# Attention and a mixture of experts on one core: the weights that turn values into gate products, made per pair of heads or per batch

## The chip, the cores and the metric

The kernel runs on one core of a Trainium2 chip. The metric is the time of one execution on the device, in microseconds (us). Five engines work side by side, each on its own queue of instructions: TensorE (PE; its weight loads are listed as PEld), VectorE (DVE), ScalarE (ACT), GpSimd (POOL) and SyncE (SP), which here only issues DMAs. Matrix products land in PSUM, in tiles that belong to tags with a fixed number of buffers each; the other engines read them there.

## The reference

Two operations in a row. The first is attention over 8 batches, 8 heads, 576 positions of 64 numbers, with rotated queries and keys:

```python
q_rot, k_rot = (rotate(q), rotate(k))
scores = scale * np.matmul(q_rot, k_rot.transpose(0, 1, 3, 2))
attn = np.exp(scores - np.max(scores, axis=-1, keepdims=True))
attn = attn / (np.sum(attn, axis=-1, keepdims=True) + 1e-09)
x = np.matmul(attn, v)            # to (8*576, 8*64) = (4608, 512) rows
```

The second sends each of the 4608 rows through a dense feed-forward part and through the one of eight experts that a gate names:

```python
logits = x @ w_gate               # (4608, 8)
expert_idx = np.argmax(logits, axis=1)
gate_w = softmax(logits)[row, expert_idx]
out = relu(x @ w1_dense) @ w2_dense
out[row] += gate_w * (relu(x @ w1[e]) @ w2[e])      # e = expert_idx[row]
```

The gate is linear in the attention's output, so it can be applied to the values before the attention weights are: the attention over (values times gate) gives the logits.

## The kernel before

**Pairs, batches, steps.** Two heads are worked on together: a pair. A batch has four pairs (`HP`), the whole attention 32 (`NP`). `attention()` (L657) runs 33 steps, i=0 to 32, each with nine parts t=0 to 8 (L692-693). In step i three pairs are under way:

- `s1_block(i+2, t)`: the scores of pair i+2 by rows of queries (L366), of which VectorE takes the negated row maximum `negm` (L368). Tag s1, two buffers.
- `s2_strip(i, t)`: the scores of pair i, transposed (L389), and their exponential on ScalarE into `pm` (L399). At the end of the step `s2_tails` does the same for the last 64 queries (L386, and an exponential). Tag s2, two buffers.
- `av_part(i-1)`: the product of the exponentials and the values of pair i-1 (L421), ten parts over t=1 to 8, into the PSUM tile `av` (one buffer). At t=8 `av_scale` divides by the row sums on VectorE: `rz` (L432), `xn` (L433), `lw` (L435) and, with the last pair of a batch, so at the end of steps with i%4=0, the sum `lgs` (L438). Its end is also what `av`'s next user, the next step's first part, waits for.

The instructions stand on each engine in just the order in which this loop writes them. Nothing is moved by a scheduler; every engine waits in its queue for what its first instruction needs.

**The row maximum** must be inside the exponent of the transposed scores. `shift_rows(i+1)` (t=1) turns `negm` on TensorE into a tag s2 tile (L374), writes it as two bf16 rows `mT` (ScalarE and VectorE), and SP copies these as rows 126 and 127 into `qT` (L379). There the first strip of the next step needs them.

**Queries and keys.** GpSimd rotates a pair's queries and keys at t=2 of the step five ahead (`stage_rope`, L311 to L314), a transposing DMA turns them into `qT` at t=2 of the step four ahead (`stage_transpose`, L324), and at t=2 of the step three ahead `stage_keys` (L349) lets SP copy the keys' half of `qT` to `kx` (L352), of which there are four buffers. `s1_block` reads `kx` first, one step after that. The raw rows come by `stage_load` at t=2, a quarter of a batch's main rows in each step, in the batch two ahead.

**Values.** The tile `v16s[b % 2]` holds for each of four pairs and five groups of 128 positions, for each of two heads: the values in fp16 (64 columns), two columns that count ones, and 16 columns of gate products: value times gate, as a high part of 8 and a low part of 8 (the high part's rounding). Making them takes these steps:

- `stage_v(b+1)` at t=5 of the batch's first step (i%4=0): SP loads the values of the next batch into `vf`, which has one buffer (L263, and the tails at L266).
- `cast_v(b, u)`: ScalarE copies pair u of them to fp16 (L270). Two casts stand in a step with i%4=0 (t=1 and t=4), one in those with i%4=2 and 3 (t=3), none with i%4=1; the last batch's lie in steps 26 and 27.
- `v_turn(i+1)` at t=5 of every step: TensorE transposes the five groups of the next pair into a tag s2 tile (L277), ScalarE copies it to `vT` (L279).
- `v_gate(i)` at t=1: ten matmuls of `vT` and the gate (high and low part, `wgb`) into free columns of the `av` tile (L287).
- `v_split(i)` at t=2: ScalarE writes the high part into `v16s` (L296), VectorE the low part, the product less the high part (L297). The product of pair i with its values starts at t=1 of the next step, so both are there by then; but they read the `av` tile, and `av_part` of the pair before goes on in the same tile at t=3.

**Other DMAs at t=5.** `x_store(b)` (L115) stores the batch's rows `xn` to DRAM in the steps with i%4=1. The ten weight loads of the second operation stand in GpSimd's queue in the steps `WS`, those of 6 to 23 with i%4=2 and 3.

**The end.** Steps 27 to 31 also route the rows of the first six batches to experts, on VectorE and GpSimd; at step 30 the first rows are gathered (`draw`, L825). From about 323 us on follows the second operation (`ffn`, L895), which the change does not touch.

Of the kernel before, what the change touches and what calls it, by code (L numbers as in the profile page):

```python
# [25 lines left out]
def kernel(  # L26
# [234 lines left out]

    def stage_v(b):
# [10 lines left out]
    def v_turn(p):  # L273
        b, u = divmod(p, HP)
        ps = pp.tile([P, 5, P], fp16, tag="s2", bufs=2, name="vps")
        for n in range(5):
            nc.tensor.transpose(ps[:, n], v16s[b % VB][:, u, n, VA:VA + 2 * D], ident_h)  # L277
        vT = ap.tile([P, 5, P], fp16, tag="vT", bufs=2, name="vT")
        nc.scalar.copy(vT, ps)  # L279
        state["vT", p] = vT  # L280

    def v_gate(p):
        vw = state["av"][:, 1, 5 * VC:5 * VC + 10 * E]
        vT = state.pop(("vT", p))
        for n in range(5):
            for x in range(2):
                nc.tensor.matmul(vw[:, 2 * E * n:2 * E * (n + 1)], lhsT=vT[:, n], rhs=wgb[:, p % HP, x],  # L287
                                 start=(x == 0), stop=(x == 1))
        state["vw", p] = vw

    def v_split(p):

        b, u = divmod(p, HP)
        vw = state.pop(("vw", p)).rearrange("p (n h e) -> p h n e", h=2, e=E)
        hi, lo = (both(v16s[b % VB][:, u, :, r * E:(r + 1) * E], VC + WB) for r in range(2))
        nc.scalar.copy(hi, vw)  # L296
        nc.vector.tensor_tensor(lo, vw, hi, AL.subtract)  # L297
# [359 lines left out]
    def attention():  # L657
# [29 lines left out]
        WS = [i for i in range(6, 24) if i % HP in (2, 3)]  # L687
# [3 lines left out]
        state["av"] = av_tile(0)  # L691
        for i in range(NP + 1):  # L692
            for t in range(9):
# [9 lines left out]
                if t == (7 if i == 0 else 5) and i + 1 < NP:  # L703
                    v_turn(i + 1)
                if i == 0 and t == 2:
                    v_turn(0)
                if i == 0 and t in (3, 5):
                    cast_v(0, 2 + t // 5)
                if i < NP:
                    t0 = 4 if i == 0 else 1  # L710
                    if t == t0:
                        v_gate(i)
                    if t == t0 + 1:
                        v_split(i)
# [4 lines left out]
                if t == 2 and i + KA < NP:  # L719
                    stage_keys(i + KA, nc.sync)  # L720
                if t == 2 and i + LA < NP:
                    stage_transpose(i + LA)
                    nb, m = divmod(i - 1, HP)
                    if 2 <= nb + 2 < B:
                        stage_load(nb + 2, m // 2 * 2, m // 2 * 2 + 2, m % 2, (0, HP) if m < 2 else ())
# [272 lines left out]
```

## Time and profile before

| | us |
|---|---|
| median of three runs | 473.59 |
| lowest, highest | 472.63, 475.58 |
| the profiled execution | 475.16 |
| its span in the trace | 473.4 |

The rows of the profile name an engine, a line, an operation, and what it writes and reads (out<-in by the program's names, with the shape), then how many, the busy time and the mean of one; behind the last bar stands the idle time of the engine before them and what ended most of it. In a timeline each line is one instruction or a few alike (x2, x10): its start, its length, and in brackets how long its engine had waited and for what.

Over the span TensorE is busy for 87%, VectorE for 73%, GpSimd for 72% and ScalarE for 62%. In forty slices of 11.8 us each (busy tenths; the clock granted to TensorE in tenths):

```profile
PE   1787998998988998998888979788999999999992
DVE  7887899999989999999899998943478323232341
ACT  6587787887877887887786875674433133332320
POOL 1899999897998989977997978745266444663232
PEclk9999999999999999999999997999999999999996
```

Attention fills the slices to about the 27th: there VectorE is at 80 to 90% or more, TensorE often not. Behind it, TensorE is at 90% or more to the end. The mean of the clock is 0.985.

### The profile page before, as it was taken

Reading aid. Unit: us, or ns where it says so; the run is one execution under the profiler, and the core shown is the slowest. Engines: PE = TensorE matmul, PEld = TensorE weight load, DVE = VectorE, ACT = ScalarE, POOL = GpSimd, SP = SyncE. Lnnn points to the kernel's source line nnn. Section 1 sums busy time; section 2 is a strip of 40 time slices with the busy share of each in tenths; the row PEclk is TensorE's granted clock in tenths of the full one; section 3 lists DMA queues with packets and bytes.
Section 4 is the critical chain, followed back from the end, with each engine's and each line's share of the span. In section 5 each row is a group of like instructions: output and inputs, shape, how many; then the busy total and the mean of one; then the engine's idle time right before and its main releaser. Section 6 shows DMA issues by size and latency. Waiting matters only on the chain.

```text
span 473.4 us, 11393 instructions
## 1 busy us (share of the span) xinstructions
PE 409.8 (87%) x4256; PEld 255.4 (54%) x4256; DVE 343.9 (73%) x651; ACT 293.9 (62%) x589; POOL 342.8 (72%) x279
## 2 busy tenths in 40 slices
PE   1787998998988998998888979788999999999992
PEld 1345665665655665665665656464445544444550
DVE  7887899999989999999899998943478323232341
ACT  6587787887877887887786875674433133332320
POOL 1899999897998989977997978745266444663232
PEclk9999999999999999999999997999999999999996
DMA  6877648779789779879779639938654556543121
GB/s 186 222 164 156 163 107 223 180 144 237 210 153 242 198 135 245 200 143 249 210 140 230 122 56 199 204 80 183 86 159 134 115 146 155 157 125 123 67 91 69
DMA packets 114124, 75.82 MB, mean 160 GB/s; under 512 B 73332, under 2 KB 107636, under 8 KB 114068
## 3 DMA queue, kind: packets, MB, share of 16 engines
q1 hardware_dynamic: 99556, 51.07, 46.6%
q0 software_dynamic: 14240, 23.73, 23.2%
q8 instruction: 36, 0.59, 0.5%
q10 hardware_dynamic: 272, 0.26, 0.2%
q14 instruction: 20, 0.16, 0.1%
HBM read 52.05 MB, written 14.42 MB: 140 GB/s over the span
## 4 chain that ended last, share of the span: by engine, by line
PE 50%; DVE 24%; DMA 12%; ACT 8%; issue 4%; SPq 1%; POOLq 0%; POOL 0%; DVEq 0%
DVE negm L368 14%; DMA kx<-qT 8%; PE py L885 7%; PE py L883 7%; PE pe L865 7%; PE pd L856 6%; PE av L421 6%; PE s L366 6%; ACT pm L399 5%; PE s L389 4%; DVE xn L433 3%; PE s L362 2%; ACT v L270 2%; PE tr L874 2%; PE s L386 1%
## 5 line engine op out<-in xcount | busy, mean ns | idle before, releaser
L368 DVE TENSOR_REDUCE negm<-s 128x1 f32<-128x576 f32 x288 | 209.9, 750 | 22.3 <-PE s L366 17.1
L399 ACT ACTIVATE pm<-s 128x512 f16<-128x512 f32 x288 | 168.4, 598 | 63.9 <-PE s L389 47.4
L366 PE MATMUL s<-kx,qT 126*128 126x288 bf16 x512 | 108.2, 294 | 21.0 <-DVE negm L368 10.0
L421 PEld LDWEIGHTS <-pm 128*128 128x128 f16 x1600 | 86.9, 98 | 63.0 <-issue 34.6
L389 PE MATMUL s<-qT,kx 128*128 128x64 bf16 (+1 forms) x512 | 109.7, 286 | 2.9 <-ACT pm L399 1.5
L421 PE MATMUL av<-v,pm 128*128 128x82 f16 x1600 | 100.4, 200 | 8.7 <-DVE v L297 8.6
L311 POOL TENSOR_TENSOR ra<-qk,cosx 128x1152 bf16<-128x1152 f32 x30 | 78.8, 2626 | 28.5 <-DVE nat L314 10.7
L888 POOL DMA_INDIRECT out_dram<-y,put_i x37 | 37.9, 1024 | 64.3 <-DVE y L887 42.8
L314 POOL TENSOR_TENSOR nat<-ra,rb 128x1152 bf16<-128x1152 bf16 x30 | 70.9, 2363 | 2.3
L366 PEld LDWEIGHTS <-qT 126*128 126x128 bf16 x512 | 40.4, 99 | 37.6 <-issue 27.4
L887 DVE COPY y<-py 128x512 f32<-128x512 f32 x37 | 25.6, 691 | 42.1 <-PE py L885 42.1
L868 ACT ACTIVATE hn<-pe,gp 128x512 bf16<-128x512 f32 x37 | 25.4, 686 | 46.1 <-PE pe L865 45.3
L820 POOL DMA_INDIRECT xg<-xd,take_i x37 | 36.8, 994 | 20.8 <-issue 9.8
L858 ACT ACTIVATE hd<-pd 128x512 bf16<-128x512 f32 (+1 forms) x40 | 22.6, 565 | 44.8 <-PE py L883 37.8
L876 DVE COPY he<-tr 128x512 bf16<-128x512 bf16 x37 | 15.6, 422 | 38.1 <-PE tr L874 38.1
L312 POOL TENSOR_TENSOR rb<-qk,sinx 128x576 bf16<-128x576 f32 x30 | 42.1, 1403 | 0.0
L313 POOL TENSOR_TENSOR rb<-qk,sinx 128x576 bf16<-128x576 f32 x30 | 42.0, 1398 | 0.0
L389 PEld LDWEIGHTS <-kx 128*128 128x128 bf16 x512 | 35.0, 97 | 8.0 <-issue 1.0
L856 PE MATMUL pd<-xs,w1d 128*128 128x512 bf16 (+1 forms) x160 | 38.0, 363 | 1.3 <-DMA xs<-xg 1.3
L865 PE MATMUL pe<-w1e,xs 128*128 x148 | 38.0, 379 | 0.9 <-PE pd L856 0.6
L883 PE MATMUL py<-w2d,hd 128*128 128x512 bf16 x148 | 38.0, 379 | 0.0
L885 PE MATMUL py<-w2e,he 128*128 x148 | 38.0, 379 | 0.0
(180 smaller groups left out, 484.6 us busy)
## 6 DMA issues: line engine op xcount, KB each, us to landing
vf<-in_v_dram SPq DMA_DIRECT2D x8, 1024.0 KB
qk<-in_q_dram SPq DMA_DIRECT2D x15, 512.0 KB
qk<-in_k_dram SPq DMA_DIRECT2D x15, 512.0 KB
kx<-qT SPq DMA_DIRECT2D x30, 144.0 KB
xd<-xn SPq DMA_DIRECT2D x8, 512.0 KB
w1e<-in_moe_w_dram POOLq DMA_DIRECT2D x8, 512.0 KB, 6.2
w2e<-in_moe_w_dram POOLq DMA_DIRECT2D x8, 512.0 KB, 13.0
vf<-in_v_dram SPq DMA_DIRECT2D x16, 64.0 KB
```

Of the source, the lines that this page charges most:

```text
L311: eng.tensor_tensor(a, x, cx, AL.mult)
L312: eng.tensor_tensor(s[:, :, :, 0:half], x[:, :, :, half:D], sx[:, :, :, 0:half], AL.mult)
L314: eng.tensor_tensor(nat.rearrange("p c w d -> p w c d"), a, s, AL.add)
L366: nc.tensor.matmul(ps[:, c, 0:CH], lhsT=qT[:, t * P:(t + 1) * P], rhs=kT[:, k0 + c * CH:k0 + (c + 1) * CH], start=True, stop=True)
L368: nc.vector.tensor_reduce(state["negm", i][:, t:t + 1], ps[:, :, 0:CH], axis=AX.XY, op=AL.max, negate=True)
L389: nc.tensor.matmul(out_ap, lhsT=kT[:, s * P:(s + 1) * P], rhs=qT[:, qa if s < 4 else qb], start=True, stop=True)
L399: nc.scalar.activation(state["pm", i][:, ORDER.index(s), 0:MAIN], ps, AF.Exp, scale=float(scale))
L421: nc.tensor.matmul(state["av"][:, h, x * VC:(x + 1) * VC], lhsT=state["pm", i][:, 4 * h + n if n < 4 else 8, q0:q0 + P], rhs=v16s[b % VB][ ...
L856: nc.tensor.matmul(ps[:, 0:n], lhsT=w1d[:, dt, ft * P:(ft + 1) * P], rhs=xs[:, 0:n, dt, :], start=(dt == 0), stop=(dt == DT - 1))
L865: nc.tensor.matmul(ps, lhsT=xs[:, u, dt, :], rhs=w[:, 0, dt, :], start=(dt == 0), stop=(dt == DT - 1))
L883: nc.tensor.matmul(py, lhsT=hd[:, ft, u], rhs=w2d[:, ft, :], start=(ft == 0), stop=False)
L885: nc.tensor.matmul(py, lhsT=he[:, ft], rhs=w[:, 0, ft, :], start=False, stop=(ft == FT - 1))
```

## The change

- The gate products of a batch's four pairs are made together, at the end of the step with i%4=0, ahead of the batch's first product with values: forty matmuls into a tag s2 tile of their own, then one copy (ScalarE) and one subtraction (VectorE) for all four pairs, 320 numbers a row in place of four times 80. For the first batch they are made in two halves, at the end of steps 0 and 1. `vT` is now one tile with room for four pairs, with one buffer in place of two.
- So the casts and turns of a batch must be over by t=4 of its step with i%4=0. They are put, by pair, at (i%4, t): (1,6) and (1,8); (2,3) and (2,5); (3,3) and (3,5); (0,2) and (0,4). Batch 1's first turn is at (2,1) instead, batch 7's third and fourth cast stand in step 27. Every step now has one cast and one turn.
- The keys' copy is at t=0 in place of t=2, from step 2 on.
- The raw rows of batches 3 to 7 are loaded one step earlier than before, their tails partly in a step of their own; those of batch 2 as before but for the split of their tails.
- `xn` is stored in the steps with i%4=3 in place of 1 (the seventh batch's in step 29 still).
- The weights are loaded in the steps of 5 to 22 with i%4=1 and 2.

```diff
+    def stage_tails(b, part):
+        load_tails(state["qk", b][:, part], (q, k)[part][b], 0, HP)
...
-    def v_turn(p):
-        b, u = divmod(p, HP)
+    def v_turn(b, u):
+        if u == 0:
+            state["vT"] = ap.tile([P, HP, 5, P], fp16, tag="vT", bufs=1, name="vT")
         ps = pp.tile([P, 5, P], fp16, tag="s2", bufs=2, name="vps")
         for n in range(5):
             nc.tensor.transpose(ps[:, n], v16s[b % VB][:, u, n, VA:VA + 2 * D], ident_h)
-        vT = ap.tile([P, 5, P], fp16, tag="vT", bufs=2, name="vT")
-        nc.scalar.copy(vT, ps)
-        state["vT", p] = vT
-
-    def v_gate(p):
-        vw = state["av"][:, 1, 5 * VC:5 * VC + 10 * E]
-        vT = state.pop(("vT", p))
-        for n in range(5):
-            for x in range(2):
-                nc.tensor.matmul(vw[:, 2 * E * n:2 * E * (n + 1)], lhsT=vT[:, n], rhs=wgb[:, p % HP, x],
-                                 start=(x == 0), stop=(x == 1))
-        state["vw", p] = vw
-
-    def v_split(p):
-
-        b, u = divmod(p, HP)
-        vw = state.pop(("vw", p)).rearrange("p (n h e) -> p h n e", h=2, e=E)
-        hi, lo = (both(v16s[b % VB][:, u, :, r * E:(r + 1) * E], VC + WB) for r in range(2))
-        nc.scalar.copy(hi, vw)
-        nc.vector.tensor_tensor(lo, vw, hi, AL.subtract)
+        nc.scalar.copy(state["vT"][:, u], ps)
+
+    def v_gate(u0):
+        if "vw" not in state:
+            state["vw"] = pp.tile([P, HP * 5, 2 * E], f32, tag="s2", bufs=2, name="vw")
+        for u in range(u0, u0 + 2):
+            for n in range(5):
+                for x in range(2):
+                    nc.tensor.matmul(state["vw"][:, 5 * u + n], lhsT=state["vT"][:, u, n], rhs=wgb[:, u, x],
+                                     start=(x == 0), stop=(x == 1))
+
+    def v_part(b, r, u0=0, u1=HP):
+        vw = (state["vw"] if r == 0 else state.pop("vw"))[:, 5 * u0:5 * u1].rearrange("p n (h e) -> p h n e", h=2)
+        hi, lo = (both(v16s[b % VB][:, u0:u1, :, y * E:(y + 1) * E].rearrange("p u n e -> p (u n) e"), VC + WB)
+                  for y in range(2))
+        if r == 0:
+            nc.scalar.copy(hi, vw)
+        else:
+            nc.vector.tensor_tensor(lo, vw, hi, AL.subtract)
...
-        WS = [i for i in range(6, 24) if i % HP in (2, 3)]
+        WS = [i for i in range(5, 23) if i % HP in (1, 2)]
...
-        state["av"] = av_tile(0)
+        loads = {}
+        for b in range(2, B):
+            n = (b - 2) * HP
+            for at, f, *x in ((n, stage_load, b, 0, 2, 0, ()), (n + 1, stage_load, b, 0, 2, 1, ()),
+                              (n + 1, stage_tails, b, 0), (n + (1 if b == 2 else 2), stage_tails, b, 1),
+                              (n + 2, stage_load, b, 2, 4, 0, ()), (n + 3, stage_load, b, 2, 4, 1, ())):
+                loads.setdefault(at + (1 if b == 2 else 0), []).append((f, *x))
+        V0 = (0, 2), (0, 7), (1, 3), (1, 5)
+        v_steps = {}
+        for b in range(1, B):
+            n = b * HP
+            for u, (c, r) in enumerate((((n - 3, 6), (n - 3, 8)), ((n - 2, 3), (n - 2, 5)), ((n - 1, 3), (n - 1, 5)), ((n, 2), (n, 4)))):
+                if b == B - 1 and u > 1:
+                    c = (n - 1, 1 + 3 * (u - 2))
+                v_steps.setdefault(c, []).append((cast_v, b, u))
+                v_steps.setdefault((n - 2, 1) if b == 1 and u == 0 else r, []).append((v_turn, b, u))
...
-                if t == (7 if i == 0 else 5) and i + 1 < NP:
-                    v_turn(i + 1)
-                if i == 0 and t == 2:
-                    v_turn(0)
                 if i == 0 and t in (3, 5):
                     cast_v(0, 2 + t // 5)
-                if i < NP:
-                    t0 = 4 if i == 0 else 1
-                    if t == t0:
-                        v_gate(i)
-                    if t == t0 + 1:
-                        v_split(i)
+                if (i, t) in V0:
+                    v_turn(0, V0.index((i, t)))
+                if i < NP and (i, t) in v_steps:
+                    for f, *x in v_steps.pop((i, t)):
+                        f(*x)
...
-                if t == 2 and i + KA < NP:
+                if t == (0 if i > 1 else 2) and i + KA < NP:
                     stage_keys(i + KA, nc.sync)
                 if t == 2 and i + LA < NP:
                     stage_transpose(i + LA)
-                    nb, m = divmod(i - 1, HP)
-                    if 2 <= nb + 2 < B:
-                        stage_load(nb + 2, m // 2 * 2, m // 2 * 2 + 2, m % 2, (0, HP) if m < 2 else ())
-                if i % HP != 1 and (t in (1, 4) if i % HP == 0 else t == 3):
-                    u = 2 + t // 4 if i % HP == 0 else i % HP - 2
-                    if 1 <= (i + 2) // HP < B and i < NP - 6:
-                        cast_v((i + 2) // HP, u)
-                if i in (NP - 6, NP - 5) and t in (1, 4):
-                    cast_v(B - 1, 2 * (i - NP + 6) + t // 4)
+                if t == 2:
+                    for f, *x in loads.pop(i, ()):
+                        f(*x)
                 if t == 5:
...
-                    if i % HP == 1 and i > HP:
+                    if i % HP == 3 and HP < i < NP - HP or i == NP - 3:
                         x_store(i // HP - 1)
...
             if i < NP:
                 s2_tails(i, 1)
-        assert not steps
+            if i in (0, 1) or i < NP and i % HP == 0:
+                u0, u1 = (2 * i, 2 * i + 2) if i < 2 else (0, HP)
+                for u in range(u0, u1, 2):
+                    v_gate(u)
+                for r in range(2):
+                    v_part(i // HP, r, u0, u1)
```

More of the change, by code (lines that the diff above doesn't have):

```diff
@@ L767, in attention @@
                 s2_tails(i, 1)
-        assert not steps
+            if i in (0, 1) or i < NP and i % HP == 0:
[4 more added lines that the diff above has]
+                    v_part(i // HP, r, u0, u1)
+        assert not steps and not v_steps and not loads
         x_store(B - 1)
```

## The prediction

> **What bounds the kernel now.** I read the page first, then the busy time of single steps, then the waits and the order of instructions inside a step.
>
> ```profile
> span 473.4 us, 11393 instructions
> PE 50%; DVE 24%; DMA 12%; ACT 8%; issue 4%; SPq 1%; POOLq 0%; POOL 0%; DVEq 0%
> ```
>
> The chain of waits lies half on TensorE, a quarter on VectorE. The change touches only the attention part, to about 323 us; behind it TensorE runs without a break, so what attention gains or loses should reach the end whole. The table of stretches, cut at the `xn` scaling that ends each step, for steps 15, 16 and 17 (columns PE, PEld, DVE, ACT, POOL busy, granted clock, DMA share, GB/s):
>
> ```profile
> 163.68:172.13 8.45, 7.95 (x108) 5.59 (x107) 7.90 (x14) 7.24 (x16) 6.47 (x5) 1.00 0.95 179
> 172.13:180.95 8.82, 7.99 (x108) 5.60 (x107) 7.96 (x14) 7.63 (x17) 8.72 (x6) 1.00 0.66 130
> 180.95:190.75 9.80, 7.95 (x108) 5.59 (x107) 9.22 (x15) 6.64 (x15) 8.67 (x6) 1.00 1.18 255
> ```
>
> TensorE does the same 7.95 us everywhere; steps differ by what holds it up. Call a batch's four steps A (i%4=0), B, C, D. A plain step (C, D) takes 8.45, A takes 8.82 (it has two casts), B takes 9.80 (the batch's `lgs` sum on VectorE). The view of waits names the two holds that the change aims at:
>
> ```profile
> PE s L366 <- DMA kx<-qT: 8.9, 8, 2.2
> PE av L421 <- DVE v L297: 8.6, 28, 0.5
> ```
>
> **The change, part by part.** Inside a plain step, in order of time (start, length, engine, line):
>
> ```profile
> 163.44 0.21 DVE L432 RECIPROCAL rz<-av 128x10 f32<-128x10 f32 x1
> 164.66 1.41 DVE L368 TENSOR_REDUCE negm<-s 128x1 f32<-128x576 f32 x2
> 164.97 0.40 PE L287 MATMUL av<-wgb,vT 128*128 128x16 f16 x10
> 165.22 0.27 PE L374 MATMUL mps<-ident_f,negm 128*9 128x128 f32 x1
> 165.46 0.40 PE L366 MATMUL s<-kx,qT 126*128 126x288 bf16 x2
> 166.53 0.38 PE L389 MATMUL s<-qT,kx 128*128 128x512 bf16 x1
> 167.16 0.34 PE L421 MATMUL av<-v,pm 128*128 128x82 f16 x5 [0.25 <-DVE v L297]
> 169.71 0.38 PE L389 MATMUL s<-qT,kx 128*128 128x512 bf16 x1
> 169.92 0.35 PE L421 MATMUL av<-v,pm 128*128 128x82 f16 x5
> ```
>
> *Ten gate matmuls leave each step.* They take 165.22-164.97=0.25 us, but the scores that follow at t=2 (165.46) need the first `negm`, done at about 164.66+0.71=165.37: VectorE takes the place of the gate. I take 0; at most 0.25.
>
> *The wait for the split leaves.* Strip to values takes 0.21 us at t=6 (169.71 to 169.92), 0.63 at t=3: the wait costs 0.42, more than the printed 0.25, as matmul ends are modelled. Behind it, the next `negm` (t=2's, ended before the split started) is ready, so I take 0.42; in steps 3 to 26 that is 24x0.42=10.1 us. Low end 24x0.25=6.0.
>
> *One cast in every step.* A had two: 8.82-8.45=0.37, in steps 4, 8, 12, 16, 20, 24, 26: +2.6 (0 to 2.6).
>
> *Keys' copy at t=0.* It goes to SP two strips earlier. On SP it may stand until the step before has ended its tails, whose keys share its buffer; queued behind it are its step's two `mT` writes, the transpose and the loads, all due a step or more later but the first. The stalls that were not under B's longer VectorE wait:
>
> ```profile
> 47.60 0.40 PE L366 MATMUL s<-kx,qT 126*128 126x288 bf16 x2 [2.17 <-DMA kx<-qT]
> 118.75 0.41 PE L366 MATMUL s<-kx,qT 126*128 126x288 bf16 x2 [0.20 <-DMA kx<-qT]
> 136.81 0.40 PE L366 MATMUL s<-kx,qT 126*128 126x288 bf16 x2 [1.23 <-DMA kx<-qT]
> 227.37 0.41 PE L366 MATMUL s<-kx,qT 126*128 126x288 bf16 x2 [0.96 <-DVE lw L435]
> 244.69 0.40 PE L366 MATMUL s<-kx,qT 126*128 126x288 bf16 x2 [0.49 <-DMA kx<-qT]
> ```
>
> The first stays (its copy is issued in step 1, where t=2 is kept). At 227.37 `lw` had long ended, so I count it as a copy too. 0.20+1.23+0.96+0.49=2.9. Late next are the `mT` rows, now behind the copy in the same queue and needed at the same step's beginning: I give back 1.0 (0 to 2.9). Net +1.9.
>
> *The gates at B's beginning.* Forty take 4x0.25=1.0 us and lie in the wait that VectorE's sum makes there:
>
> ```profile
> 72.84 0.21 DVE L432 RECIPROCAL rz<-av 128x10 f32<-128x10 f32 x1
> 74.17 1.32 DVE L438 TENSOR_REDUCE lgs<-lw 128x40 f32<-128x640 f32 x1
> 76.21 0.41 PE L366 MATMUL s<-kx,qT 126*128 126x288 bf16 x2 [1.31 <-DVE negm L368]
> L433 DVE TENSOR_TENSOR xn<-av,rz 128x640 bf16<-128x640 f32 x32 | 26.4, 824 | 1.1
> L297 DVE TENSOR_TENSOR v<-av,v 128x80 f16<-128x80 f32 x32 | 7.6, 239 | 4.4 <-ACT v L296 3.5
> L270 ACT CAST v<-vf 128x640 f16<-128x640 f32 x32 | 23.1, 721 | 0.0
> L279 ACT COPY vT<-vps 128x640 f16<-128x640 f16 x32 | 22.0, 689 | 0.3 <-PE vps L277 0.3
> ```
>
> But the subtraction of four pairs (320 elements) now stands behind `lgs`, ahead of B's first `negm`. Between 239 ns (80) and 824 (640) it is 0.24+240/560x0.585=0.49, about 0.07 overlapped: -0.42 in each of steps 5, 9, ..., 25: -2.5 (0.2 to 0.8 each). The high part, on ScalarE, runs while TensorE does B's first scores and costs nothing unless it outlasts `lgs`.
>
> *B's cast at t=6, its turn at t=8.* ScalarE must now do a cast before the exponentials of strips 7 and 8, and a copy of 0.69 between them and the tails, and the two buffers of tag s2 make TensorE's turn, tails and next strips wait for these in a row. By the queue, TensorE reaches t=2 of C 0.1 us later than before although B saved 0.42: -0.5 a batch, six times: -3.0 (0 to 0.72+0.69=1.4 each).
>
> Steps 3 to 26: 10.1+2.6+1.9-2.5-3.0=+9.1.
>
> *The beginning.* The first cast of batch 1 moves from step 2, t=3, to step 1, t=6, and there its values haven't landed:
>
> ```profile
> 38.98 0.54 SPq L263 DMA_DIRECT2D vf<-in_v_dram  x1
> 42.75 4.71 DMA kx<-qT
> 43.31 1.85 ACT L399 ACTIVATE pm<-s 128x512 f16<-128x512 f32 x3
> 43.00:45.00 2.00, 1.96 (x30) 1.52 (x29) 1.98 (x3) 1.95 (x4) 1.95 (x1) 1.00 1.18 301
> 46.70:47.50 0.80, 0.00 (x0) 0.00 (x0) 0.00 (x0) 0.00 (x0) 0.80 (x1) 1.00 1.08 205
> ```
>
> The load is issued at 38.98; the engines move it until 45.0 at least; the copy behind it lands at 42.75+4.71=47.46, its burst starting at 46.7. So the values land between 45.0 and 47.46; I take 46.7. ScalarE reaches the cast at about 43.9, after the first of the three exponentials, and everything queued behind stands: exponentials 7 and 8, the tails, the high part. Cast 0.66, two exponentials of 0.55, half of the tails, twenty gates of 0.5: TensorE starts step 2 at 49.4 in place of 47.60. With batch 1's extra turn at t=1 and the split before it, less what step 2 saves itself: -2.2 (0 if landed at 45.0, -3.0 at 47.46).
>
> *The clock.* TensorE then idles from about 44.75 to 48.0. What such a hole does shows here (same columns):
>
> ```profile
> 282.00:285.40 3.40, 1.71 (x25) 1.23 (x25) 3.26 (x9) 1.36 (x3) 3.06 (x5) 1.00 0.98 132
> 285.40:288.80 3.40, 2.68 (x23) 1.76 (x23) 3.30 (x11) 1.42 (x3) 2.74 (x7) 0.50 1.13 177
> 288.80:292.20 3.40, 3.40 (x29) 2.27 (x26) 2.10 (x7) 1.31 (x3) 3.20 (x6) 0.50 1.22 208
> 292.20:295.60 3.40, 3.14 (x40) 2.26 (x39) 3.08 (x6) 2.95 (x7) 3.09 (x8) 1.00 1.23 217
> ```
>
> After a stretch in which TensorE was busy for 1.71 of 3.40 us the granted clock was 0.50 for 6.8 us, and a full stretch did 29 matmuls in place of 40: 27% lost, up to 6.8x0.27=1.8 us. However stretches of 3.4 us are laid over the new hole, one has under 1.7 us of work. I take -1.6 (0 to -1.8). [...]
>
> *The end.* Steps 27 to 29 are VectorE's (routing), where the split's 0.2 us each goes and 0.42 comes once: +0.3 (-0.5 to +1.5). What steps 30 and 31 save ends at the gather of rows, which starts from VectorE's work at step 30's beginning. Loads a step earlier give POOL back waits, but POOL is not on the chain; `xn`'s store, moved from B to D, and the weights are needed only after step 29.
>
> Sum: 9.1-2.2-1.6+0.3=5.6 us. The profiled execution took 475.16 (1.8 around its span), the median of the three runs is 473.59; the half-clock stretch may be this execution's own, so I take the sum from the median: 468.0.
>
> **The rivals.**
>
> *Slower: batches of values land late every time.* Before, the first cast of a batch had a whole step more. In the batch of step 12:
>
> ```profile
> 99.80 0.82 DVE L433 TENSOR_TENSOR xn<-av,rz 128x640 bf16<-128x640 f32 x1
> 106.86 0.79 SPq L263 DMA_DIRECT2D vf<-in_v_dram  x1
> 113.79 4.82 DMA kx<-qT
> ```
>
> The load left 7.06 us into A. With A at 8.0 it leaves at about 6.9; t=6 of B, with its `lgs` ahead, comes some 8.3 us into B, so the cast is reached 1.1+8.3=9.4 us after the issue. The copy of keys behind the load landed at 113.79+4.82=118.61, 11.75 us after it: a bound for the values too. If every batch is so, ScalarE stands up to 11.75-9.4=2.35 us in six steps: +14.1, 482.1. It decides from 9.4 us on; slower by 1% takes 478.3-468.0=10.3, or 1.7 us a batch, a landing after 11.1. Against it: the weights, which left in C and D and shared the DMA engines with that load, leave in B and C now. Chance 0.11.
>
> *The gain of the wait is eaten.* ScalarE or VectorE takes the split's place after t=3: without the 10.1 the time is 478.1, with half of it 473.0. VectorE's 7.90 busy of 8.45 speaks for it, 0.24 of it leaving against. 0.22.
>
> *No hole at the beginning*, or the clock stays up through it: 468.0-1.6=466.4 with the clock alone, 464.2 with both. For it: values that landed by 45.0, and only one hole in the trace to judge the clock by. 0.22. [...]
>
> *POOL becomes the bound*: busy 6.47+8.72+8.67=23.9 of 27.1 us; four steps of the forecast take about 34.5 against some 32. 0.03, near 470.
>
> **How the numbers follow.** Forecast 0.42, spread about 468 from 466.4 to 471, four fifths of it under 468.85 (1%, about what a measurement of this kernel tells from no change). Faster: 0.34 and 0.22 make 0.56; same: 0.08, 0.22 and 0.03 make 0.33; slower 0.11. The range of 8 in 10 takes in the forecast, most of the third case, the lower half of the eaten gain and the bounds of the first terms: 463 to 474. The forecast's own is 466.4 to 471.
>
> **What would show it.** Right: plain steps of 8.0 us, A too; B near 9.9; no wait of L421 on the split; no stall for keys after 47; ScalarE waiting for values in step 1, and a clock of 0.5 in step 2. Wrong: a cast waiting for values in later batches, plain steps over 8.2, a C step that begins late by over a microsecond.

## The result, and the profile after

The changed kernel takes 471.82 us (median of 20 runs, 468.01 to 478.37), the kernel before 475.37 (20 runs, 472.32 to 481.15). The ratio is 0.9921, with a 95% interval from 0.9892 to 0.9950: 3.8 us faster, 2.4 to 5.1. The forecast was 5.6 us and 468.0; the time lies in its range, 463 to 474, but the gain is under the 1% that was held likeliest. Of the 3.8 us between 468.0 and 471.82, 1.8 come from the kernel before, for which the forecast took 473.59, the median of three runs.

The page of the changed kernel: span, chain of waits, and the group of the value products, the last column of which was their wait for the split.

```profile
span 469.4 us, 11334 instructions
PE 61%; DVE 17%; DMA 8%; ACT 6%; issue 3%; SPq 2%; POOLq 0%; POOL 0%; ACTq 0%; DVEq 0%
L424 PE MATMUL av<-v,pm 128*128 128x82 f16 x1600 | 100.6, 201 | 0.0
```

The span is 4.0 us shorter. VectorE's share of the chain of waits fell from 24% to 17% and TensorE's rose from 50% to 61%; the value products wait for nothing any more. The table of stretches, cut at the start of the `rz` row that ends each step, gives steps 13 to 16 (B, C, D, A; columns as before):

```profile
147.08:156.52 9.44, 8.12 (x124) 5.88 (x124) 9.20 (x17) 6.67 (x15) 9.26 (x7) 1.00 0.92 231
156.52:165.58 9.06, 8.50 (x109) 6.09 (x109) 7.92 (x14) 8.00 (x16) 8.13 (x5) 1.00 0.92 192
165.58:173.63 8.05, 7.75 (x96) 5.43 (x96) 7.60 (x14) 7.04 (x15) 6.05 (x4) 1.00 1.13 198
173.63:181.59 7.96, 7.66 (x96) 5.38 (x96) 7.47 (x14) 6.97 (x15) 7.80 (x5) 1.00 0.76 209
```

A batch took 8.81+9.80+8.45+8.45=35.51 us and takes 34.51 now: A 0.85 less, D 0.40 less, B 0.36 less, but C 0.61 more. The beginning, by ScalarE's and TensorE's timeline of the changed kernel:

```profile
47.02 0.73 ACT L273 CAST v<-vf 128x640 f16<-128x640 f32 x1 [2.72 <-DMA vf<-in_v_dram]
48.29 0.39 PE L392 MATMUL s<-qT,kx 128*128 128x64 bf16 x8 [3.17 <-ACT pm L402]
49.91 0.64 PE L369 MATMUL s<-kx,qT 126*128 126x288 bf16 x2
```

ScalarE stands for 2.72 us before batch 1's first cast, and TensorE begins step 2 at 49.91 in place of 47.60. In the same trace, stretches of 3.41 us (TensorE's busy time first, the granted clock third from the right):

```profile
45.30:48.70 3.40, 0.39 (x8) 0.35 (x8) 1.42 (x4) 1.68 (x3) 3.32 (x3) 1.00 0.78 107
48.70:52.10 3.40, 2.99 (x34) 2.07 (x35) 1.59 (x3) 1.80 (x6) 3.32 (x3) 0.50 0.67 196
52.10:55.50 3.40, 3.26 (x24) 2.06 (x23) 1.22 (x4) 1.85 (x4) 3.32 (x2) 0.50 0.00 1
76.00:79.42 3.42, 2.46 (x56) 1.99 (x53) 3.35 (x7) 2.05 (x5) 3.34 (x2) 1.00 0.95 322
79.42:82.83 3.41, 3.41 (x27) 2.31 (x26) 2.58 (x5) 1.41 (x3) 3.33 (x3) 0.50 1.14 337
```

The clock is halved for two stretches in step 2, as forecast, and for one more in step 5, where nobody expected it: TensorE had been busy for 72% of the stretch before.

Both kernels were run and traced a second time, on another chip (see the experiments). There the times show no gain clear of noise: the ratio is 0.9988 (0.9935 to 1.0041). What the change saves, by stretch of the program, in us, with the lengths from one `rz` row to another:

| | forecast | first traces | second traces |
|---|---|---|---|
| to step 1's end | 0 | -0.4 | -0.8 |
| step 2 | -3.8 | 10.54 to 14.84: -4.3 | 10.55 to 11.46: -0.9 |
| steps 3 to 26 | +9.1 | 216.1 to 210.0: +6.1 | 217.3 to 209.2: +8.1 |
| steps 27 to 32 | +0.3 | 51.7 to 48.9: +2.8 | 55.4 to 57.9: -2.5 |
| behind them | 0 | -0.2 | -0.2 |
| span | 5.6 | 4.0 | 3.7 |

### The profile page after: what moved, and what is told of

Same layout as the page of the kernel before. It is cut to its first block, busy times and chain, and to the rows that moved or that the text cites. A ratio compares the mean times of both kernels' runs of the same rounds, so it can differ in the third digit from the quotient of the medians.

```text
span 469.4 us, 11334 instructions
## 1 busy us (share of the span) xinstructions
PE 411.6 (88%) x4241; PEld 258.5 (55%) x4256; DVE 338.8 (72%) x628; ACT 293.3 (62%) x566; POOL 343.5 (73%) x279
## 4 chain that ended last, share of the span: by engine, by line
PE 61%; DVE 17%; DMA 8%; ACT 6%; issue 3%; SPq 2%; POOLq 0%; POOL 0%; ACTq 0%; DVEq 0%
DVE negm L371 9%; PE s L369 9%; PE s L392 8%; PE av L424 7%; PE pd L869 7%; PE pe L878 7%; PE py L898 7%; PE py L896 7%; ACT pm L402 3%; DMA kx<-qT 2%; PE vps L281 2%; PE s L365 2%; PE tr L887 2%; DVE lgs L441 2%; PE s L389 2%
## 5 line engine op out<-in xcount | busy, mean ns | idle before, releaser
L371 DVE TENSOR_REDUCE negm<-s 128x1 f32<-128x576 f32 x288 | 204.5, 749 | 18.8 <-PE s L369 17.0
L896 PE MATMUL py<-w2d,hd 128*128 128x512 bf16 x141 | 36.5, 379 | 0.4
```

Source lines behind the costliest of these rows:

```text
L371: nc.vector.tensor_reduce(state["negm", i][:, t:t + 1], ps[:, :, 0:CH], axis=AX.XY, op=AL.max, negate=True)
L896: nc.tensor.matmul(py, lhsT=hd[:, ft, u], rhs=w2d[:, ft, :], start=(ft == 0), stop=False)
```

## The experiments

A, B, C, D are a batch's steps; a ratio is to the kernel before on the same chip. The changed kernel was run for the result and in after_again only, so where the ratio of another experiment is set beside its 0.9921, that compares across chips, which differ (0.9921 and 0.9988). Each experiment has one trace, and line numbers are those of its own kernel. The expectations of before_keys0, first_two and weights_late give a late step the number of the pair whose products end in it, one less than the loop's i; the text here uses i.

**turn_next**: is it the place of B's turn that costs C its microsecond?

```diff
-                v_steps.setdefault((n - 2, 1) if b == 1 and u == 0 else r, []).append((v_turn, b, u))
+                v_steps.setdefault((n - 2, 1) if u == 0 else r, []).append((v_turn, b, u))
```

> The first turn of each batch (b=2 to 7) moves from the last part of its B step to t=1 of the C step behind it; the cast stays at t=6 of B. Account A (the turn and its copy of vT stand between the last strips and the tails, which share the two buffers of tag s2, so TensorE waits 0.3 us before the turn and 0.4 us behind it and does the turn's 0.3 us with nothing beside it): C steps fall from 9.06 us to about 8.3 (8.1 to 8.5), A, B and D stay at 7.96, 9.44 and 8.05; six batches gain 4 to 5 us, so a ratio to the kernel before of about 0.983. Account B (it is the cast at t=6, which delays the exponentials of strips 7 and 8): C steps stay above 8.8, ratio 0.992.

The stretches of a B and a C step, and VectorE's row at the beginning of another C:

```profile
180.22:189.66 9.44, 8.12 (x125) 5.85 (x125) 9.19 (x16) 6.67 (x15) 9.28 (x6) 1.00 0.80 228
189.66:198.76 9.10, 8.62 (x109) 6.07 (x109) 7.82 (x14) 8.11 (x16) 9.00 (x6) 1.00 0.93 174
158.56 0.28 DVE L380 TENSOR_TENSOR mT<-mps,mT 9x128 bf16<-9x128 f32 x1 [0.82 <-ACT mT L379]
```

C is 9.10, no better than 9.06: account A fell. TensorE's wait of 0.40 us behind the turn, ahead of the last part of the tails, is down to 0.10, but VectorE stands 0.82 us, since ScalarE now does the turn's copy ahead of `mT`. Account B's number came, but its cause, the cast, stands where it stood and isn't tested here. The ratio is 0.9891 (0.9806 to 0.9977), no different from the change's.

**t5_t7**: the same turn in B, where VectorE is late anyway, with its cast one part earlier. Two more changes go with it: batch 1's first cast and turn stand in step 2, and the values are loaded at t=3.

```diff
-            for u, (c, r) in enumerate((((n - 3, 6), (n - 3, 8)), ((n - 2, 3), (n - 2, 5)), ((n - 1, 3), (n - 1, 5)), ((n, 2), (n, 4)))):
+            for u, (c, r) in enumerate((((n - 3, 5), (n - 3, 7)), ((n - 2, 3), (n - 2, 5)), ((n - 1, 3), (n - 1, 5)), ((n, 2), (n, 4)))):
...
+                if b == 1 and u == 0:
+                    c, r = (n - 2, 2), (n - 2, 3)
                 v_steps.setdefault(c, []).append((cast_v, b, u))
-                v_steps.setdefault((n - 2, 1) if b == 1 and u == 0 else r, []).append((v_turn, b, u))
+                v_steps.setdefault(r, []).append((v_turn, b, u))
...
+                if t == (3 if i else 5) and i % HP == 0 and i // HP + 1 < B:
+                    stage_v(i // HP + 1)
                 if t == 5:
...
-                    if i % HP == 0 and i // HP + 1 < B:
-                        stage_v(i // HP + 1)
```

> The changed kernel with batch 1's first cast and turn in step 2 (t=2, t=3), the values' loads at t=3 of step A in place of t=5 (batch 1's as they were), and the first cast and turn of batches 2 to 7 at t=5 and t=7 of B in place of t=6 and t=8. Account A (the second turn costs 1.0 us only where it stands at a step's border or in a step without slack; inside B VectorE is late anyway and hides it): C steps 8.05 to 8.3, B 9.44 to 9.7, no wait for values; step 2 ends at 56.2; in all 8 to 10 us under the changed kernel, ratio near 0.975. Account B (a turn more than one a step costs ScalarE's 0.69 and TensorE's 0.3 wherever it stands): B rises to 10.2 or more as C falls to 8.05; only the start's 4 us and batch 2's wait are gained, ratio 0.982 to 0.985.

```profile
180.65:190.80 10.15, 8.65 (x133) 6.29 (x133) 9.29 (x17) 7.34 (x16) 9.91 (x6) 1.00 0.87 243
190.80:199.09 8.29, 8.05 (x104) 5.68 (x102) 7.83 (x15) 7.32 (x15) 8.19 (x6) 1.00 1.06 153
```

C falls by 0.77, B rises by 0.71: account B for the turn. With the turn at three places B and C together took 18.50, 18.54 and 18.44 us, each time 0.9 to 1.1 more than 9.44 and 8.05. Step 2 ended at 57.17, batch 2's cast still waited 1.15 us, and the ratio, 0.9906 (0.9862 to 0.9950), is that of neither account.

**cast_step2**: batch 1's first cast and turn go to step 2 (the middle part of the diff above).

> Batch 1's first cast moves from step 1, t=6 to step 2, t=2, its turn to step 2, t=3; nothing else is changed. Account A (the values' landing at 47.0 held ScalarE for 2.7 us, but the mT rows and the keys' copy queued behind these values landed at 48.0 to 48.2 in the same trace and hold TensorE next): TensorE begins step 2 at 47.5 to 48.2 in place of 49.9; step 2 ends (its rz) at about 58.3 in place of 60.3 if the clock still halves, 56.7 if it doesn't. Account B (the cast's wait was all there was): TensorE begins step 2 at about 46, without a fall of the clock, and step 2 ends at about 55.9. The rest of the trace is the changed kernel's.

```profile
47.49 0.41 PE L369 MATMUL s<-kx,qT 126*128 126x288 bf16 x2
83.37 0.73 ACT L273 CAST v<-vf 128x640 f16<-128x640 f32 x1 [2.92 <-DMA vf<-in_v_dram]
81.65:85.08 3.43, 0.44 (x5) 0.41 (x6) 1.27 (x4) 1.71 (x3) 3.35 (x3) 1.00 0.91 182
85.08:88.49 3.41, 3.16 (x24) 2.08 (x23) 1.51 (x2) 2.25 (x5) 3.38 (x3) 0.50 0.56 125
```

Step 2 began at 47.49, account A's 47.5, but with no wait before it; it kept the full clock and ended at 56.2, between A's 56.7 and B's 55.9. (With the same cast, t5_t7 and weights_late did wait for keys there, 1.06 and 1.65 us, and lost a stretch to the half clock, so A's next wait exists too.) But four microseconds won made batch 2's cast, in step 5, stand 2.92 us for its values, and the clock was halved behind that. By step 8's end 1.1 us of the gain was left. Ratio 0.9876 (0.9806 to 0.9945).

**fill_hole**: work for TensorE in the hole, whose result is read by nobody.

```diff
+            if i == 1:
+                fill = pp.tile([P, 2, 512], f32, tag="s1", bufs=2, name="fill")
+                for n in range(14):
+                    nc.tensor.matmul(fill[:, n % 2], lhsT=state["qkT", 3][0][0:KM, 0:P],
+                                     rhs=state["qkT", 3][0][0:KM, 0:512], start=True, stop=True)
             if i < NP:
                 s2_tails(i, 0)
```

> Fourteen matmuls of 512 columns (about 3.0 us), whose result nobody reads, fill TensorE's wait at the end of step 1, ahead of the tails; the wait of ScalarE for the values stays. Account A (a stretch of 3.4 us with TensorE little at work halves the clock for the next two): the granted clock stays 1.00 through step 2, the tails still begin at about 48.3, and step 2 ends (its rz) at about 58.6 in place of 60.3. Account B (the low clock has another cause, such as the waits inside step 2): 0.50 in step 2 as now, and its end at 60.3 or later.

```profile
45.30:48.70 3.40, 3.40 (x23) 1.63 (x22) 2.08 (x5) 1.71 (x3) 3.32 (x3) 1.00 0.59 108
48.70:52.10 3.40, 2.74 (x47) 1.99 (x45) 1.36 (x3) 2.17 (x6) 3.32 (x3) 1.00 0.54 186
46.27 0.73 ACT L273 CAST v<-vf 128x640 f16<-128x640 f32 x1 [1.30 <-DMA vf<-in_v_dram]
48.66 0.40 PE L392 MATMUL s<-qT,kx 128*128 128x64 bf16 x8
49.09 0.71 ACT L409 ACTIVATE pm<-s 128x512 f16<-128x512 f32 x2 [1.12 <-PE s L392]
```

The clock stayed at 1.00, and step 2 ended at 58.61, account A's 58.6, 1.68 us before the changed kernel's 60.29. The half clock's price is more than that, for the values came earlier here (cast at 46.27 in place of 47.02), and the tails had to wait for the filling matmuls. From the tails' start to the end of step 2 it is 58.61-48.66=9.95 us, the same as in after_again, which kept its clock too (57.65-47.70), and 60.29-48.29=12.00 in the changed kernel's first trace: a price of 2.05, forecast at 1.6 and at most 1.8. Batch 2's cast then stood 1.2 us. Ratio 0.9915 (0.9872 to 0.9958).

**gate_pairs**: the gates back at ten a step, in `av`, with the split at t=2.

```diff
-            if i in (0, 1) or i < NP and i % HP == 0:
...
-                    v_part(i // HP, r, u0, u1)
+                if i < NP:
+                    t0 = 4 if i == 0 else 1
+                    if t == t0:
+                        gate_pair(i)
+                    if t == t0 + 1:
+                        split_pair(i)
```

> The changed kernel with its gates as before: ten matmuls a step at t=1 into free columns of av, the split at t=2; casts, turns, keys, loads as changed. Account A (TensorE's wait at t=3 for the split on VectorE is what the change takes away): steps A, C and D are longer by 0.42 us each (8.38, 9.48, 8.47), the wait of the value products on the split is back, B stays within 0.2 of 9.44 since it gains VectorE's 320 elements and loses the 80; 8 to 10 us slower than the changed kernel, ratio to the kernel before near 1.01. Account B (the wait was covered by the next row maximum, and the steps are shorter for another reason, such as casts and loads): D at 8.05 to 8.15, ratio near 0.993.

```profile
179.05:188.03 8.98, 7.86 (x106) 5.59 (x106) 7.78 (x15) 7.25 (x16) 8.82 (x5) 1.00 0.74 224
188.03:197.46 9.43, 7.37 (x94) 5.03 (x94) 9.04 (x17) 6.31 (x15) 9.33 (x6) 1.00 0.82 213
197.46:206.87 9.41, 8.71 (x119) 6.24 (x119) 8.14 (x15) 8.20 (x17) 6.36 (x5) 1.00 0.95 134
206.87:215.33 8.46, 7.95 (x106) 5.59 (x106) 7.91 (x16) 7.25 (x16) 4.28 (x3) 1.00 0.95 197
182.22 0.72 ACT L273 CAST v<-vf 128x640 f16<-128x640 f32 x1
182.83 0.23 ACT L315 CAST v<-av 128x80 f16<-128x80 f32 x1
183.38 0.34 PE L440 MATMUL av<-v,pm 128*128 128x82 f16 x5 [0.87 <-DVE v L316]
```

Account A: D is back at 8.46, C is 0.35 longer, and B is the same, for there the wait comes back and the subtraction of 320 elements (0.48 us in the changed kernel) leaves. A is 1.02 longer, 0.6 more than expected, as the last three rows show: the changed kernel's cast at t=2 now stands on ScalarE ahead of the high part, and the value products wait 0.87 us (0.42 to 0.47 in A of the kernel before, 0.25 in most other steps of both). The batch is 36.28-34.51=1.77 us longer, of which about 0.6 come from this experiment's own order on ScalarE. The ratio is 1.0073 (1.0028 to 1.0117) against the change's 0.9921. So the gates made once a batch are the largest gain of the change in its steps; that the rest of it, alone, would lose, isn't shown.

**loads_old**: loads, stores and weights in the steps they had before.

```diff
-        WS = [i for i in range(5, 23) if i % HP in (1, 2)]
+        WS = [i for i in range(6, 24) if i % HP in (2, 3)]
...
-                if t == 2:
-                    for f, *x in loads.pop(i, ()):
-                        f(*x)
+                if t == 2 and i + LA < NP:
+                    nb, m = divmod(i - 1, HP)
+                    if 2 <= nb + 2 < B:
+                        stage_load(nb + 2, m // 2 * 2, m // 2 * 2 + 2, m % 2, (0, HP) if m < 2 else ())
...
-                    if i % HP == 3 and HP < i < NP - HP or i == NP - 3:
+                    if i % HP == 1 and i > HP:
```

> The changed kernel with the loads of queries and keys, the stores of xn and the weights in the steps that they had before. Account A (the values of batch 2 land 9.2 to 9.6 us after their issue, in place of 7.0 before, since weights and loads now move beside them): they land within 8 us, and no ScalarE or TensorE wait for them at the end of step 5 over 0.5 us; the other stretches (7.96, 9.44, 9.06, 8.05) are unchanged, waits for keys and mT rows come back by 1 to 3 us. Account B (that batch's values land late in any order): the wait at the end of step 5 is there with over 1 us.

Two batches' values, SP's issue and ScalarE's cast:

```profile
106.41 0.75 SPq L266 DMA_DIRECT2D vf<-in_v_dram  x1
117.66 0.73 ACT L273 CAST v<-vf 128x640 f16<-128x640 f32 x1 [1.12 <-DMA vf<-in_v_dram]
214.46 0.97 SPq L266 DMA_DIRECT2D vf<-in_v_dram  x1
226.92 0.73 ACT L273 CAST v<-vf 128x640 f16<-128x640 f32 x1 [2.45 <-DMA vf<-in_v_dram]
```

Batch 2's cast has no wait, as account A has it. But batches 3, 5 and 6 have, by 1.12, 1.43 and 2.45 us, and the ratio is 0.9985 (0.9934 to 1.0036). Without its new places for loads, stores and weights the change has the late values of the slower rival, though in three batches and not in six, and shows no gain. The rival's deadline is seen here: ScalarE reached the casts at 116.54 and 224.47, 10.1 and 10.0 us after the issue (9.4 in the forecast), and the values were there 11.25 and 12.46 us after it.

**keys_t2** and **before_keys0**: the keys' copy by itself, taken out and put in.

```diff
-                if t == (0 if i > 1 else 2) and i + KA < NP:
+                if t == 2 and i + KA < NP:
```

> The keys' copy goes back to t=2 in every step; everything else as in the changed kernel. Account A (the copy at t=0 is what took TensorE's waits for keys away): such waits come back, 1 to 3 us in all in steps 3 to 24, and the time rises by as much; steps without one keep 8.05. Account B (the loads, stores and weights in other steps took them away): no wait for keys over 0.3 us, and the time of the changed kernel within 0.5 us in the steps.

> The kernel before with the keys' copy at t=0 from step 2 on and nothing else. Account A (the copy stood too late in SP's queue): the waits for keys in steps 11, 21 and 23 (1.23, 0.96 and 0.49 us) leave, at most half comes back as waits for the mT rows now behind it; plain steps keep 8.45; 1 to 3 us faster, ratio 0.994 to 0.998. Account B (what the copy waits for, the turned keys, lands late wherever the copy stands): the waits stay or move to the mT rows, no gain, ratio within 0.002 of 1.

In keys_t2, 3.3 us of waits for keys are back in steps 3 to 26 (2.4 named so, 0.9 put down to a `lw` long done), and these steps take 212.9 us, 2.9 more than in the first trace of the changed kernel; 1.45 without batch 2's late values in the one and the half clock of step 5 in the other. In before_keys0 the waits for keys leave from step 3 on, and a new one comes, for the `mT` rows behind the copy in SP's queue:

```profile
245.59 0.38 PE L389 MATMUL s<-qT,kx 128*128 128x512 bf16 x1 [1.95 <-DMA qT<-mT]
```

Its steps 3 to 26 take 216.6, between the two traces of before (216.1 and 217.3): nothing gained there. But one step, the 24th, took 11.72 of them (9.27 and 9.44 in the two traces of before), with the wait above and the clock halved behind it:

```profile
243.31:246.72 3.41, 1.46 (x22) 0.88 (x23) 2.01 (x4) 1.03 (x4) 3.39 (x3) 1.00 0.73 149
246.72:250.13 3.41, 3.41 (x32) 2.25 (x30) 2.22 (x5) 2.59 (x6) 3.41 (x2) 0.50 0.99 181
```

The other 23 steps took 204.9, in place of 206.8 and 207.8: a gain of 1.9 and 2.9, which this one step undid. The times are on the side of a gain in one run and of none in the other: before_keys0 has 0.9917 (0.9882 to 0.9952), 2 to 6 us of gain; and keys_t2 has 0.9913 (0.9865 to 0.9962), no slower than the change. One trace of each can't settle that; what the copy is worth stays open between nothing and the whole 0.8%, and it doesn't add up with the rest.

**after_again** and **before_again**: the two kernels once more, unchanged. They and first_two ran on a chip on which the kernel before takes 482.25.

> The changed kernel once more, for a second trace. Account A (what repeats is the kernel's, what doesn't is the execution's): steps of 7.96, 9.44, 9.06 and 8.05 and the wait for values in step 1 repeat within 0.3 us; the half clock in step 5, which followed a stretch in which TensorE was 72% busy, falls elsewhere or is missing, since its stretches lie otherwise in the step. Account B: it is there again at the same place, and so belongs to the gates.

> The kernel before once more, for a second trace. Account A: steps of 8.45, 8.81 and 9.80 repeat; the waits for keys (1.23, 0.96, 0.49 and 0.20 us in the first trace) lie in other steps and come to 1 to 5 us in all, which is where the spread of its times comes from; the half clock of step 28 may be missing. Account B: the waits for keys repeat in the same steps with the same lengths, and the spread has another cause.

Steps of 7.96, 9.44, 9.07 and 8.05 repeat, and 8.45, 8.81 and 9.80; so do the waits for keys of the kernel before, in other steps but with a like sum (7.3 and 6.6 us in steps 3 to 26). In the changed kernel the casts of batch 1 and 2 waited 1.39 and 0.78 us, and the clock kept full speed through both places. The half clock of step 5 is missing, so it is not in every execution; but loads_old and weights_late have such a one too, each in another B, behind just such stretches, 56 or 57 matmuls of which 40 are gates:

```profile
143.72:147.13 3.41, 2.50 (x56) 1.85 (x53) 3.34 (x7) 1.73 (x5) 3.19 (x2) 1.00 1.16 149
147.13:150.54 3.41, 3.01 (x23) 2.04 (x23) 2.24 (x4) 1.76 (x4) 1.68 (x1) 0.50 1.09 349
215.86:219.27 3.41, 2.45 (x57) 2.02 (x55) 3.34 (x7) 2.11 (x5) 3.33 (x2) 1.00 1.02 342
219.27:222.68 3.41, 3.41 (x25) 2.19 (x25) 2.55 (x6) 1.41 (x3) 3.33 (x4) 0.50 0.74 189
```

It seems to belong to the gates and to how the stretches happen to lie over them: in the ten traces with gates made together, 50 stretches of the clock's beat hold all forty, and the half clock followed three of them, those with 2.45 (twice) and 2.50 us of TensorE's work. They are the least busy of the fifty but for one of 2.49 (at 291.04 in the changed kernel's first trace), which kept the full clock. What sets the three apart isn't shown. It made a B of 10.78 out of one of 9.44, 1.34 us, in step 5 of the changed kernel and in step 21 of weights_late. On this chip the kernels' step 31 took 12.1 (before) and 13.8 us (changed) in place of 6.7 and 6.1, with waits of ScalarE and TensorE to which the profile gives no releaser on their own core (up to 1.85 us before, up to 3.9 changed). Step 31 alone cost the changed kernel 1.7 us more than the kernel before, and the ratio there is 0.9988 (0.9935 to 1.0041), though the steps up to 26 gained more than in the first traces.

**first_two** and **weights_late**: can the beginning be mended? The one puts batch 2's first cast into C too, the other (with batch 1's as in cast_step2) starts the weights in step 9.

```diff
+                if b < 3 and u == 0:
+                    c, r = (n - 2, 2), (n - 2, 3)
                 v_steps.setdefault(c, []).append((cast_v, b, u))
-                v_steps.setdefault((n - 2, 1) if b == 1 and u == 0 else r, []).append((v_turn, b, u))
+                v_steps.setdefault(r, []).append((v_turn, b, u))
```

```diff
-        WS = [i for i in range(5, 23) if i % HP in (1, 2)]
+        WS = [i for i in range(9, 27) if i % HP in (1, 2)]
```

> The changed kernel with the first cast and turn of batches 1 and 2 in the C step (t=2 and t=3) in place of B's t=6 and t=8 (batch 1's turn stood at t=1 of C); the other batches as changed. Account A (values that are late only for these two batches: 2.7 us in step 1 and, in four of the traces so far, 1.1 to 3.3 us at the end of step 5): no ScalarE wait for values anywhere, step 2 ends at 56.2 to 57.2 in place of 60.3, the step behind it 9.1 to 9.5 without a wait before it; time of step 7's end 108.5 to 111, 2 to 4 us under the changed kernel in all, ratio near 0.985. Account B (the rotation of queries and keys on GpSimd and what is queued behind its results on SP set the time by step 7): step 7 still ends at 111 to 112.5 with TensorE waiting for mT rows or keys, ratio 0.99 as for the changed kernel.

> The changed kernel with batch 1's first cast and turn in step 2 (t=2 and t=3) and the ten weight loads in the steps of 9 to 26 with i%4=1 and 2, in place of 5 to 22: none beside batch 2's values and the mT rows of steps 5 to 7. Account A (the start's gain was eaten at steps 6 to 8 by transfers that the first two weight loads slow): step 2 ends at 56.2 to 57.2, no wait over 0.5 us in steps 5 to 8, step 7 ends at 107 to 109.5 in place of 112.6 (first trace) and 110.3 (second); attention 3 to 5 us under the changed kernel, ratio near 0.985 on a chip like the first. Account B (the rotation on GpSimd sets that time, whatever the weights do): step 7 ends at 110.5 or later.

In first_two no cast waits, step 2 ends at 56.5 and step 6 at 91.6, but in step 8 TensorE stands 2.46 us for keys and it ends at 111.35: account B. Ratio 0.9977 (0.9938 to 1.0016), the changed kernel's on that chip. Its step 5 is a B with neither a cast nor a turn of the next batch:

```profile
72.53:81.97 9.44, 8.33 (x131) 6.14 (x131) 9.19 (x16) 6.57 (x15) 9.28 (x7) 1.00 1.12 270
```

It takes 9.44 like the B's that have the cast, so B pays nothing for the cast by itself.

In weights_late step 2 ended at 58.2 with a half clock, batch 2's cast waited 0.57, steps 7 and 8 had no wait, and step 8 ended at 110.67, 1.9 before the first trace of the changed kernel, but after the second (110.27). The number is account B's (110.5 or later), the cause is not: the time was lost in step 6, which took 11.05 with a half clock in it where 9.06 is usual. Its ratio, 0.9862 (0.9807 to 0.9917), is the lowest seen, but six runs don't part it from the change's 0.9921.

## Why the prediction was right, and where it wasn't

*The wait for the split.* Right in mechanism and size: 0.40 in D against 0.42. In gate_pairs a batch loses 1.77 us, about 1.2 without the clash in A; the forecast, with B's 0.42 taken off, is 4x0.42-0.42=1.26.

*One cast a step.* Right: A lost 0.85, which is 0.42 and 0.43 where 0.37 was named.

*The gates at B's beginning.* Right in B itself: the wait that leaves and the 320-element subtraction that comes (0.49 forecast, 0.48 measured) were to cancel, and B is 9.44 with the gates made together and 9.43 with gate_pairs. That B is 0.36 shorter than before has another reason: its turn now falls behind the cut, in C, as t5_t7 shows. What the sum didn't have is that the clock was halved behind the forty gates in three of the ten traces: 1.34 us in step 5 of the changed kernel and in step 21 of weights_late.

*B's cast and turn.* Right in kind, and too small. By the cuts of the table C now holds two turns and B none, so the two steps must be taken together: 18.25 us before, 18.33 forecast, 18.50 measured. The term of 0.5 a batch is 0.67, 1.0 us more in six batches. The prediction followed the queue to t=2 of C only; about the same was lost wherever the turn was tried.

*Keys' copy.* The waits moved as described, `mT` rows late next. The changed kernel kept 1.2 us of waits of both kinds in steps 3 to 26 of the first trace (0.79 for keys, 0.38 for `mT` rows), where 1.0 was given back. Its worth in time stays open, as told above.

*The beginning.* Right in each step in the first trace: values at 47.0 (46.7 forecast), TensorE at 49.9 (49.4), clock 0.50, in all -4.3 for -3.8. The wait's term held (2.25 for 2.2), the clock's was too small (2.05 for 1.6). What was missed is that it differs from one execution to another: in the second trace the clock stayed up, as one of the rivals has it, and the loss was 0.9. Missed too is that mending it helps little: what step 2 wins is lost at batch 2's values, at the half clock behind them or at the keys of step 8.

*The end.* +2.8 and -2.5 in place of +0.3. Of the first, 1.7 are not the change's: a half clock in step 28 that the first trace of the kernel before had for two stretches and the second for one (12.66 and 10.94 us). But 1.1 are: steps 30 and 31 took 8.00 and 6.06 us in place of 8.48 and 6.70, and as the time behind step 32 is the same, this reached the end. The prediction had put it at nothing, as ending at the gather of rows. The second is step 31's long wait, which the profile doesn't explain.

*The signs.* Steps of 8.0 for A and D, no wait on the split, values late in step 1 and the halved clock in step 2 came in the first trace. C at 8.0, B near 9.9 and no stall for keys did not, and one sign of being wrong did: a cast of a later batch waited (0.78 us in the second trace).

*The rivals.* Late values every batch did not come, and loads_old points to the new steps of loads, stores and weights (the prediction named the weights; the three were not tried apart). Batch 2 alone was late, in most traces. The wait's gain was not eaten. GpSimd has 31.2 us of work in a batch of 34.5 (the sum of its column above) and was not seen to hold a step by itself; what holds step 8 when the beginning is faster, its late results or slow transfers, was not parted. Transfers seem to have a share: step 6 ended at 94.57 in cast_step2 and at 94.66 in weights_late, and TensorE then waited 0.73 us for keys in step 8 of the first and not at all in the second.

Taken together: steps 3 to 26 gave 6.1 and 8.1 for 9.1, and the total 3.8 for 5.6. Six batches of undisturbed steps give 6x1.00=6.0, where the forecast's terms but the keys' come to 10.1+2.6-2.5-3.0=7.2. What is left, 0.1 and 2.1 us, is what the keys' copy, late `mT` rows and the half clocks made together, against the 1.9 of the keys. So the way of the change was seen, and its parts in steps 3 to 26 were within two microseconds; the beginning and the end differ by 3 to 5 us from one pair of traces to the other, and that the sum came near is in part luck.

## What to carry to other kernels

A wait of TensorE on a value made in its own accumulator tile was worth its full length in the steps that it held up (0.40 us in D, 0.35 in C) and nothing in B, and making the value for several steps at once removed it; but look where the work that is pulled together now stands, and count what each step loses as well as what it gains. With every step already filled, moving one more copy from one step to another moved its cost with it (0.71 us more in B, 0.77 less in C). A cut between steps can also put the same work into one step or the other, so compare neighbours together before a term is judged by one of them. And a start that was made faster paid little while the next loads were ready no earlier (cast_step2: of 4.1 us won by step 2's end 1.1 were left at step 8's).

## What the runs showed of the hardware

The half clock came in whole stretches of 3.41 us at a fixed beat through a trace: in the changed kernel's first trace it stands from 48.70 to 55.53 and again from 79.42, nine stretches behind 48.70; in weights_late it falls at 86.15 and at 219.27, 39 stretches later. The busy time of the stretch before didn't decide alone. Behind 0.39 us of 3.41 (the changed kernel), 0.44 (cast_step2) and 1.72 (the kernel before, step 28) the clock was halved, but so it was behind 2.46, 2.50 and 2.45 with forty matmuls of 16 columns in them. Without such matmuls, too, it was halved behind a stretch of 1.97 in weights_late and not behind one of 1.55 in loads_old:

```profile
82.74:86.15 3.41, 1.97 (x25) 1.46 (x24) 2.16 (x6) 3.02 (x6) 3.33 (x2) 1.00 0.89 239
86.15:89.56 3.41, 3.41 (x24) 2.24 (x23) 2.44 (x4) 2.00 (x4) 3.33 (x3) 0.50 0.22 50
188.09:191.50 3.41, 1.55 (x21) 1.16 (x19) 2.80 (x6) 1.98 (x4) 3.33 (x3) 1.00 1.29 172
191.50:194.91 3.41, 2.93 (x34) 1.93 (x32) 1.77 (x4) 2.64 (x8) 3.33 (x3) 1.00 0.98 321
```

A hole of 1.84 us that the beat cut in two, 1.46 and 0.38, left the clock at 1.00, in the second trace of the changed kernel:

```profile
43.90:47.32 3.42, 1.96 (x24) 1.29 (x22) 3.19 (x6) 2.03 (x5) 3.34 (x2) 1.00 0.64 129
47.32:50.73 3.41, 2.55 (x44) 2.01 (x44) 1.11 (x4) 2.57 (x7) 3.41 (x3) 1.00 0.83 236
```
